# A second DMA queue for the stores and twiddle loads of one stage

## The chip, the cores and the metric

The kernel runs on one core of a Trainium2 chip: TensorE (PE in the profile) multiplies matrices, VectorE (DVE), ScalarE (ACT) and GpSimd (POOL) work on elements, and SyncE (SP) issues DMA transfers. ScalarE can issue them too, in the order of its own instructions. The transfers of every issuer run on the same 16 DMA engines of the core. The metric is the time of one execution on the device in microseconds.

## The reference, cut to what matters

```python
def attn(x, v, pos_emb, w1, w2):          # x, v: (2, 12480, 128); pos_emb: (12480, 64)
    h = (maximum(pos_emb @ w1, 0) @ w2) * exp(-0.01 * pos)[:, None]
    u = x * v
    U, H = rfft(u, n=2 * S, axis=1), rfft(h, n=2 * S, axis=0)
    y = irfft(U * H[None], n=2 * S, axis=1)[:, :S]
    return x * y
def moe(z, w_in, w_out):                  # z: (24960, 128); w_in: (128, 2048)
    g = z @ w_in
    return maximum(0.01 * g, g) @ w_out
out = moe(attn(...).reshape(24960, 128), moe_w_in, moe_w_out)
```

The long convolution is done by a Fourier transform of length 98 x 128, split into two short transforms with a multiplication by twiddles in the first; all of it in float32.

## The kernel before, in words

The work runs in this order: the first short transform of batch 0 and of the filter (0 to 176 us); the second transform of batch 0, the product with the filter, the way back and the preparation of the weights (176 to 357 us); then, for some 1440 us, the two matrix multiplications of the MLP over 64 tiles of tokens, with the convolution of batch 1 woven between them.

The change lies in the first part alone. It goes in 16 steps, c = 0 to 15, of four columns of the transform each (`MC = 4`). Step c does this:

- `load_a(c + 3)`: SyncE issues the load of the twiddles `ft` (L197), then x and v of batch 0 (`xt`, `vt`, through `load_tokens`, L67 and L69: one large transfer and two small ones for each). For every fourth step `load_pos` follows, with `pos` in the same way.
- The stores of step c - 1 (`store`, L287): two transfers of `o` to `scr1`, put off by one step in the list `late`, so that they stand behind the loads of step c + 3.
- `prep(c + 2)`: GpSimd multiplies x by v into `uh` (L212); VectorE and GpSimd turn `ft` by a fixed angle (L221, L235, L236) to make the second set of twiddles; TensorE transposes `pos` (L229), ScalarE copies it out (`pts`, L232), TensorE multiplies it by w1 (L240), VectorE puts the ReLU, times the window, into `uh` (L243).
- For each of the four columns: TensorE's products `a` (L314), ScalarE's copy of one half of it (`a1s`, L98), VectorE's sum and difference into `o` (L100, L102).

Buffers: `o` and `a1s` have two, `a`, `uh`, `xt` and `vt` three, `ft` five. Each engine runs its instructions in the written order, and an instruction that waits for a semaphore holds those behind it. Completions of DMA transfers are told by eight semaphores (DMAHW0 to DMAHW7) that are given out in turn over all issuers; a transfer whose semaphore is still held by an earlier one waits for that one's landing before it is issued.

At the end of the part, the last step's rows go to the tile `bin0` directly from `o` (L307), those of the other steps from `scr1` (L302), and the next part loads its tiles `bin` from `scr1` (L496), which needs every store to have landed.

The functions that the diff touches are these:

Of the kernel before, what the change touches and what calls it, by code (L numbers as in the profile page):

```python
# [20 lines left out]
MC = 4  # L21
# [6 lines left out]
def tile_conv_mlp(ctx, tc, x, v, pos_emb, w1, w2, w_in, w_out, cf, cr, cg, cb, ci, cw, out):  # L28
    nc = tc.nc
# [14 lines left out]
    scr1 = dram.tile([128, NA, 2 * C0], F32, name="scr1")  # L44
# [18 lines left out]
    def load_tokens(t, src, m0, n):  # L63

        full = src[: ROWS * NB, :].rearrange("(a p n) d -> a p n d", p=2, n=HB)
        for r in (slice(0, R0), slice(R0, ROWS)):
            nc.sync.dma_start(out=t[r], in_=full[r, :, m0:m0 + n, :])  # L67
        last = src[ROWS * NB + m0:ROWS * NB + m0 + n, :]
        nc.sync.dma_start(out=t[ROWS:], in_=last[None, None, :, :].to_broadcast([1, 2, n, last.shape[1]]))  # L69
# [24 lines left out]
    def add_sub(pool, a0, a1, dst0, dst1, view, bufs):  # L94

        a1s = pool.tile([128, 512], F32, tag="a1s", name="a1s", bufs=bufs)[:a1.shape[0]]
        n = a1.shape[1]
        nc.scalar.copy(a1s[:, :n], a1)  # L98
        yield
        nc.vector.tensor_tensor(out=dst0, in0=view(a0), in1=view(a1s[:, :n]), op=ALU.add)  # L100
        yield
        nc.vector.tensor_tensor(out=dst1, in0=view(a0), in1=view(a1s[:, :n]), op=ALU.subtract)  # L102

    def run(g):
        for _ in g:
            pass


    def chunk(c):
        k0 = c * KC  # L110
        return k0, min(KC, NA - k0)
# [46 lines left out]
    with tc.manual_schedule():  # L158
# [3 lines left out]
        def fetch_a(c):  # L162
            ft = s0.tile([128, MC1 * 4 * NA], F32, tag="s0", name="ft1", bufs=3)[:NA].rearrange(
                "a (m p e) -> a m p e", m=MC1, p=2)
            nc.sync.dma_start(out=ft, in_=cf[:, c * MC1:(c + 1) * MC1])
            xv = []
            for i, src in enumerate((x, v)):
                t = s0.tile([128, 1024], F32, tag=f"s{1 + i}", name="xv1", bufs=3 - i)[:NA, :2 * MC1 * D].rearrange(
                    "a (p m d) -> a p m d", p=2, d=D)
                load_tokens(t, src[1], c * MC1, MC1)  # L170
                xv.append(t)
            got[c] = ft, xv
# [3 lines left out]
        def mult_a(c):  # L176
            ft, (xt, vt) = got.pop(c)
            nc.gpsimd.tensor_tensor(out=xt, in0=xt, in1=vt, op=ALU.mult)
            u1[c] = ft, xt

        with ExitStack() as st:
# [9 lines left out]
            def load_pos(q):  # L191
                pos_t[q] = sba.tile([NA, 2, PQ, FO], F32, tag="pos", name="pos")
                load_tokens(pos_t[q], pos_emb, q * PQ, PQ)

            def load_a(c):
                ft = sba.tile([NA, MC, 2 * NA], F32, tag="ft", name="ft", bufs=5)
                nc.sync.dma_start(out=ft, in_=cf[:, c * MC:(c + 1) * MC, 0])  # L197
                xt = sba.tile([NA, 2, MC, D], F32, tag="xt", name="xt", bufs=3)
                vt = sba.tile([NA, 2, MC, D], F32, tag="vt", name="vt", bufs=3)
                load_tokens(xt, x[0], c * MC, MC)  # L200
                load_tokens(vt, v[0], c * MC, MC)
                f_t[c], xv_t[c] = ft, (xt, vt)
                if c < 2:
                    f1_t[c] = sba.tile([NA, MC, 2 * NA], F32, tag="f1", name="f1", bufs=3)
                    nc.sync.dma_start(out=f1_t[c], in_=cf[:, c * MC:(c + 1) * MC, 1])
# [45 lines left out]
            for i in range(2):  # L251
                nc.sync.dma_start(out=w1bd[64 * i:64 * i + 64, 64 * i:64 * i + 64], in_=w1)
            make_identity(nc, ident)
            load_a(0)
            nc.sync.dma_start(out=win, in_=cw)
            nc.sync.dma_start(out=rot, in_=cr)
            load_a(1)
            run(prep(0))
            load_a(2)
            run(prep(1))  # L260
            late = []
            for c in range(NC0):
                if c + 3 < NC0:
                    load_a(c + 3)
                    if (c + 3) * MC % PQ == 0:
                        load_pos((c + 3) * MC // PQ)
                if c == 2:
                    nc.sync.dma_start(out=mb, in_=cb)
                    nc.sync.dma_start(out=mi, in_=ci)
                    for s in range(2):  # L270
                        for ri in range(2):
                            nc.sync.dma_start(out=mi2[HB * s:HB * s + HB, ri], in_=ci[HB * ri:HB * ri + HB, s])
                if c == 6:
                    for m, mh, ml in ((mb.rearrange("p s r q -> p s (r q)"), mb_h, mb_l), (mi, mi_h, mi_l)):
                        nc.scalar.copy(mh, m)
                        nc.vector.tensor_tensor(out=ml, in0=m, in1=mh, op=ALU.subtract)
                for f in late:
                    f()
                late = []
                uh, ft, f1 = uh_t.pop(c), f_t.pop(c), f1_t.pop(c)  # L280
                nxt = prep(c + 2) if c + 2 < NC0 else iter(())
                o = sba.tile([NA, 2, MC, 2, C0], F32, tag="o", name="o")

                def store(m0, n, o, c=c):
                    for ri in range(2):
                        r0 = HB * ri + c * MC + m0
                        nc.sync.dma_start(out=scr1[r0:r0 + n].rearrange("m k e -> k m e"),  # L287
                                          in_=o[:, ri, m0:m0 + n].rearrange("a m s d -> a m (s d)"))
                if c == 7:
                    w22 = s0.tile([128, D], F32, tag="mi", name="w22", bufs=1)  # L290
                    for i in range(2):
                        nc.sync.dma_start(out=w22[64 * i:64 * i + 64, :], in_=w2)
                if c == NC0 - 3:
                    fetch_a(0)

                    bin0 = s0.tile([128, MC1 * 4 * NA], F32, tag="s0", name="bin0", bufs=3)[
                        :, :KC * 2 * C0].rearrange("p (k s e) -> p k s e", k=KC, s=2)

                def early():
                    for ri in range(2):  # L300
                        rows = slice(HB * ri, HB * ri + HB - DIR * MC)
                        nc.sync.dma_start(out=bin0[rows], in_=scr1[rows, :KC, :].rearrange("p k (s e) -> p k s e", s=2))  # L302

                def direct(m, o, c=c):
                    for ri in range(2):
                        r0 = HB * ri + c * MC + m
                        nc.sync.dma_start(out=bin0[r0:r0 + 1], in_=o[:KC, ri, m])  # L307
                if c == NC0 - 1:
                    mult_a(0)
                for mm in range(MC):  # L310
                    a = psa.tile([NA, 2, 512], F32, tag="a", name="a", bufs=3)
                    for p, f, n in ((0, ft, NA), (1, f1, ROWS)):
                        for ri in range(2):
                            nc.tensor.matmul(a[:, p, C0 * ri:C0 * ri + C0], f[:n, mm, NA * ri:NA * ri + NA],  # L314
                                             uh[:n, p, mm], start=True, stop=True)
                    run(add_sub(sba, a[:, 0, :2 * C0], a[:, 1, :2 * C0], o[:, :, mm, 0, :], o[:, :, mm, 1, :],
                                lambda t: t.rearrange("a (r e) -> a r e", r=2), 2))
                    next(nxt, None)
                    if c >= NC0 - DIR:
                        direct(mm, o)  # L320
                    if c == NC0 - 1 and mm == EARLY:
                        early()
                    if c == NC0 - 1 and mm == MC - 1:
                        store(0, MC, o)
                if c < NC0 - 1:
                    late.append(lambda store=store, o=o: store(0, MC, o))
# [161 lines left out]
        with ExitStack() as st:  # L488
# [111 lines left out]
            for c in range(NCH):  # L600
# [11 lines left out]
                n = chunk(c)[1]  # L612
# [234 lines left out]
```

## Time and profile before

| | |
|---|---|
| median of 3 runs | 1797.21 us (1795.04 to 1797.37) |
| the profiled execution | 1797.53 us, span 1795.5 us |
| PE, DVE, ACT, POOL busy | 95%, 54%, 50%, 33% of the span |
| first part, 0 to 176 us | PE 135.73, DVE 96.96, ACT 42.03, POOL 75.26 us busy; DMA share 0.90, 249 GB/s |

The whole-span shares are those of the long MLP part. The first part must be read alone, since other things limit it there. The DMA share is the mean busy share of the 16 DMA engines. In the rows `SPq` and `ACTq` are DMA-issuing and waiting instructions of SyncE and ScalarE, q1 is the DMA queue that SyncE issues into, q10 that of ScalarE. The tile `scr` stands for `scr1` here, and `o`, `xt` and so on leave out buffer numbers.

### The profile page before, as it was taken

The page shows a single profiled execution, that of the slowest core. Times are in us where ns is not written, and L with a number is a line of the kernel's source. Part 1 is how long each engine was busy: PE and PEld are TensorE (multiplying, and loading weights), DVE is VectorE, ACT ScalarE, POOL GpSimd, SP SyncE. Part 2 cuts the span into 40 slices and gives each one's busy share as a digit, 9 for nine tenths or more (in the row PEclk, how much of TensorE's full clock was granted, in tenths as well). Part 3 has the DMA queues.
Part 4 walks back from the last instruction along what each step waited for, and adds up shares of the span by engine and source line. Part 5 has one row for each costly group of instructions (what it writes and reads, how often), then busy time and mean ns, then how long its engine had stood idle before and what let it go on. Part 6 is the DMA issues. An engine that isn't in the chain of part 4 may idle for free.

```text
span 1795.5 us, 29288 instructions
## 1 busy us (share of the span) xinstructions
PE 1714.1 (95%) x10620; PEld 1607.7 (90%) x10620; DVE 966.5 (54%) x1688; ACT 892.5 (50%) x1803; POOL 587.2 (33%) x450
## 2 busy tenths in 40 slices
PE   6787989879999999999999999999999999999998
PEld 6677545479999999999999999999999999999998
DVE  3566788845455555555555544444444444444444
ACT  1222444324445666666666666444444444444444
POOL 3453334213323555555544444211121111211120
PEclk8789999989999999999999999999999999999999
DMA  9898999786756465555555541212211122112210
GB/s 224 244 274 259 310 301 321 235 248 192 216 159 180 121 179 142 140 144 144 144 144 144 141 129 54 77 50 65 60 50 50 54 64 57 51 50 60 65 51 14
DMA packets 147707, 251.77 MB, mean 140 GB/s; under 512 B 10842, under 2 KB 96742, under 8 KB 144492
## 3 DMA queue, kind: packets, MB, share of 16 engines
q1 hardware_dynamic: 127420, 224.21, 44.8%
q10 hardware_dynamic: 20144, 25.69, 4.3%
q8 instruction: 84, 1.38, 0.3%
q14 instruction: 59, 0.48, 0.1%
HBM read 166.37 MB, written 83.43 MB: 139 GB/s over the span
## 4 chain that ended last, share of the span: by engine, by line
PE 84%; DMA 9%; DVE 3%; SPq 2%; issue 1%; ACT 1%; POOL 0%; ACTq 0%; POOLq 0%; DVEq 0%
PE mh L693 10%; PE mh L695 10%; PE mh L694 10%; PE acc L713 10%; PE acc L712 10%; PE acc L714 10%; PE yp L679 6%; PE cv L132 4%; PE cv L350 2%; DMA scr<-o 2%; PE up L117 2%; PE dp L139 2%; DMA xt<-in_x_dram 2%; PE op L723 2%; DMA ft<-in_cf_dram 1%; PE xp L671 1%
## 5 line engine op out<-in xcount | busy, mean ns | idle before, releaser
L699 DVE SCALAR_TENSOR_TENSOR rl<-mh,rh 128x390 fp32r<-128x390 f32 x1024 | 574.9, 564 | 616.6 <-ACT rh L698 614.9
L698 ACT ACTIVATE rh<-mh 128x390 fp32r<-128x390 f32 x1024 | 508.1, 498 | 387.3 <-PE mh L695 369.9
L693 PE MATMUL mh<-zh,w_in_h 128*128 128x390 f32 x1024 | 366.0, 357 | 0.0
L695 PE MATMUL mh<-zh,w_in_l 128*128 128x390 f32 x1024 | 350.2, 342 | 0.0
L694 PE MATMUL mh<-zl,w_in_h 128*128 128x390 f32 x1024 | 349.4, 341 | 0.0
L713 PE MATMUL acc<-rl,w_out_h 128*128 128x390 f32 x1024 | 348.8, 341 | 0.0
L712 PE MATMUL acc<-rh,w_out_h 128*128 128x390 f32 x1024 | 348.3, 340 | 0.0
L714 PE MATMUL acc<-rh,w_out_l 128*128 128x390 f32 x1024 | 348.2, 340 | 0.0
L686 POOL TENSOR_TENSOR zl<-zf,zh 128x390 fp32r<-128x390 f32 x63 | 64.9, 1030 | 706.1 <-ACT zh L685 706.1
L693 PEld LDWEIGHTS mh<-zh,w_in_h 128*128 128x128 f32 x1024 | 194.0, 189 | 2.2 <-DVE rl L699 0.2
L694 PEld LDWEIGHTS mh<-zl,w_in_h 128*128 128x128 f32 x1024 | 193.9, 189 | 2.2 <-DVE zl L686 0.2
L695 PEld LDWEIGHTS mh<-zh,w_in_l 128*128 128x128 f32 x1024 | 194.0, 189 | 0.0
L713 PEld LDWEIGHTS acc<-rl,w_out_h 128*128 128x128 f32 x1024 | 193.9, 189 | 0.0
L714 PEld LDWEIGHTS acc<-rh,w_out_l 128*128 128x128 f32 x1024 | 193.1, 189 | 0.0
L712 PEld LDWEIGHTS acc<-rh,w_out_h 128*128 128x128 f32 x1024 | 193.0, 188 | 0.0
L679 PEld LDWEIGHTS yp<-g,cp 98*128 98x128 f32 x1024 | 123.5, 192 | 0.0
L679 PE MATMUL yp<-g,cp 98*128 98x97 f32 (+1 forms) x1024 | 123.1, 274 | 0.0
L431 POOL TENSOR_TENSOR us<-us,hd 128x512 f32<-128x512 f32 (+1 forms) x50 | 63.6, 1272 | 146.2 <-ACT us L429 146.2
L685 ACT CAST zh<-zf 128x390 fp32r<-128x390 f32 x64 | 33.2, 519 | 148.8 <-DVE zf L684 148.8
L485 POOL TENSOR_TENSOR cp<-cin 98x512 f32<-98x512 f32 x63 | 88.4, 1402 | 0.0
L484 POOL TENSOR_TENSOR cp<-cin 98x512 f32<-98x512 f32 x63 | 81.5, 1293 | 17.5 <-DMA cin<-scr 9.4
L98 ACT COPY a1s<-a 98x384 f32<-98x384 f32 x64 | 30.6, 479 | 110.3 <-PE a L314 67.2
(129 smaller groups left out, 2149.9 us busy)
## 6 DMA issues: line engine op xcount, KB each, us to landing
cin<-scr SPq DMA_DIRECT2D x63, 392.0 KB
hd<-hspec SPq DMA_DIRECT2D x48, 512.0 KB
g<-in_cg_dram SPq DMA_DIRECT2D x64, 300.1 KB
scr<-o SPq DMA_DIRECT2D x32, 588.0 KB
bin<-scr SPq DMA_DIRECT2D x23, 768.0 KB
scr1b<-o SPq DMA_DIRECT2D x32, 392.0 KB
hspec<-hs ACTq DMA_DIRECT2D x48, 256.0 KB
scr<-ct ACTq DMA_DIRECT2D x24, 512.0 KB
```

The source lines that it names most:

```text
L132: nc.tensor.matmul(dst, u, w, start=(i == 0), stop=(i == 2))
L484: eng.tensor_tensor(out=o1, in0=c0, in1=c1, op=ALU.subtract)
L485: eng.tensor_tensor(out=o0, in0=c0, in1=c1, op=ALU.add)
L679: nc.tensor.matmul(yp[:, at:at + n], ci_t[:, r, m, p, :], g[:, r, p, m, :n], start=(r == 0), stop=(r == 1))
L693: nc.tensor.matmul(hp, w_in_h[:, fs], zh, start=True, stop=False)
L694: nc.tensor.matmul(hp, w_in_h[:, fs], zl, start=False, stop=False)
L695: nc.tensor.matmul(hp, w_in_l[:, fs], zh, start=False, stop=True)
L698: nc.scalar.activation(out=rh, in_=hp, func=AF.Relu)
L699: nc.vector.scalar_tensor_tensor(out=rl, in0=hp, scalar=0.0, in1=rh, op0=ALU.max, op1=ALU.subtract)
L712: nc.tensor.matmul(ap, w_out_h[:, f, :], rh, start=False, stop=False)
L713: nc.tensor.matmul(ap, w_out_h[:, f, :], rl, start=False, stop=False)
L714: nc.tensor.matmul(ap, w_out_l[:, f, :], rh, start=False, stop=(f == NF - 1))
```

## The change

```diff
@@ load_a(c)
                 ft = sba.tile([NA, MC, 2 * NA], F32, tag="ft", name="ft", bufs=5)
-                nc.sync.dma_start(out=ft, in_=cf[:, c * MC:(c + 1) * MC, 0])
+                nc.scalar.dma_start(out=ft, in_=cf[:, c * MC:(c + 1) * MC, 0])
@@ store(m0, n, o, c=c)
                         r0 = HB * ri + c * MC + m0
-                        nc.sync.dma_start(out=scr1[r0:r0 + n].rearrange("m k e -> k m e"),
+                        nc.scalar.dma_start(out=scr1[r0:r0 + n].rearrange("m k e -> k m e"),
                                           in_=o[:, ri, m0:m0 + n].rearrange("a m s d -> a m (s d)"))
```

ScalarE issues 48 transfers that SyncE issued: 16 loads of `ft` and 32 stores. Everything else of the part stays with SyncE: x, v, pos, the second twiddles of steps 0 and 1 (`f`, L205), and constants. The instructions of TensorE, VectorE and GpSimd keep their order; the numbers of the semaphores they wait for change.

SyncE's order before, from the load of `ft` for step 8 to the stores of step 4:

```order
L197 DMA ft<-in_cf_dram 98x4x196 [waits DMAHW2_49,PE_49]
L67 DMA xt<-in_x_dram 96x2x512 [waits DMAHW3_49,Pool_49]
L67 DMA xt<-in_x_dram 1x2x512 [waits DMAHW4_49]
L69 DMA xt<-in_x_dram 1x2x512 [waits DMAHW5_49]
L67 DMA vt<-in_v_dram 96x2x512 [waits DMAHW6_49]
L67 DMA vt<-in_v_dram 1x2x512 [waits DMAHW7_49]
L69 DMA vt<-in_v_dram 1x2x512 [waits DMAHW0_49]
L67 DMA pos<-in_pos_emb_dram 96x2x1024 [waits DMAHW1_49]
L67 DMA pos<-in_pos_emb_dram 1x2x1024 [waits DMAHW2_49]
L69 DMA pos<-in_pos_emb_dram 1x2x1024 [waits DMAHW3_49]
L287 DMA scr_60<-o 98x4x384 [waits DMAHW4_49,DVE_49]
L287 DMA scr_60<-o 98x4x384 [waits DMAHW5_49]
```

SyncE's order now, from the load of x for step 8 to that for step 9:

```order
L67 DMA xt<-in_x_dram 96x2x512 [waits DMAHW2_49,Pool_49]
L67 DMA xt<-in_x_dram 1x2x512 [waits DMAHW3_49]
L69 DMA xt<-in_x_dram 1x2x512 [waits DMAHW4_49]
L67 DMA vt<-in_v_dram 96x2x512 [waits DMAHW6_49]
L67 DMA vt<-in_v_dram 1x2x512 [waits DMAHW0_49]
L69 DMA vt<-in_v_dram 1x2x512 [waits DMAHW2_49]
L67 DMA pos<-in_pos_emb_dram 96x2x1024 [waits DMAHW3_49,PE_49]
L67 DMA pos<-in_pos_emb_dram 1x2x1024 [waits DMAHW4_49]
L69 DMA pos<-in_pos_emb_dram 1x2x1024 [waits DMAHW5_49]
L67 DMA xt<-in_x_dram 96x2x512 [waits DMAHW0_49,Pool_49]
```

Of the twelve issues of such a step the load of `ft` and the two stores are gone; none of SyncE's waits in the step is for VectorE any more.

ScalarE's order in a later step without pos, as a piece of the difference (`pts` is the copy of the transposed pos, `a1s` that of a product):

```order
-L98 COPY a1s<-a 98x384 [waits DVE_49,PE_49,Activation_49] x4
+L98 COPY a1s<-a 98x384 [waits PE_49,Activation_49]
+L98 COPY a1s<-a 98x384 [waits DVE_49,PE_49,Activation_49] x2
+L197 DMA ft<-in_cf_dram 98x4x196 [waits DMAHW4_49,Pool_49]
+L287 DMA scr_60<-o 98x4x384 [waits DMAHW6_49,DVE_49]
+L287 DMA scr_60<-o 98x4x384 [waits DMAHW0_49]
+L98 COPY a1s<-a 98x384 [waits PE_49,Activation_49]
 L232 COPY pts<-pt 128x392 [waits PE_49]
```

Three issues now stand between the copy of a step's fourth product and that of the next step's first; the first store waits for VectorE, and each waits for an earlier transfer.

## Rows read from the trace of the kernel before

**Rows 1.** Timeline, VectorE: start us, us, engine, line, operation, out<-in, [idle before <-releaser].
```profile
43.00 0.56 DVE L100 TENSOR_TENSOR o<-a,a1s 98x384 f32<-98x384 f32 x1 [2.01 <-DMA scr<-o]
...
65.29 0.56 DVE L100 TENSOR_TENSOR o<-a,a1s 98x384 f32<-98x384 f32 x1 [2.57 <-DMA scr<-o]
...
70.56 0.54 DVE L102 TENSOR_TENSOR o<-a,a1s 98x384 f32<-98x384 f32 x1
...
86.60 0.56 DVE L100 TENSOR_TENSOR o<-a,a1s 98x384 f32<-98x384 f32 x1 [6.46 <-DMA scr<-o]
...
147.79 0.56 DVE L100 TENSOR_TENSOR o<-a,a1s 98x384 f32<-98x384 f32 x1 [2.59 <-DMA scr<-o]
```

**Rows 2.** Chain of waits from 43 to 147.8 us: shares by engine and line.
```profile
by line: DMA scr<-o 25.9%; DMA ft<-in_cf_dram 23.7%; PE a L314 14.4%; DMA xt<-in_x_dram 9.4%; DMA pos<-in_pos_emb_dram 7.7%; DMA vt<-in_v_dram 6.9%; SPq L67 4.6%; issue 3.0%; DVE o L102 3.0%; SPq L272 2.2%; PE hp L240 2.2%; DVE q L221 1.7%;
```

**Rows 3.** Busy time by stretch, as the first row names the columns.
```profile
core 0: us, PE busy (x) PEld busy (x) DVE busy (x) ACT busy (x) POOL busy (x), PEclk, DMA share, GB/s
...
43.00:147.80 104.80, 84.80 (x492) 77.67 (x490) 64.73 (x124) 26.12 (x57) 54.52 (x34) 0.85 0.93 262
```

**Rows 4.** Waits from 43 to 147.8 us: us in total, times, longest us.
```profile
DVE o L100 <- DMA scr<-o: 40.3, 11, 8.1
```

**Rows 5.** Timeline, SyncE's DMA issues around step 4's store.
```profile
68.67 0.33 SPq L197 DMA_DIRECT2D ft<-in_cf_dram  x1
...
74.03 2.48 SPq L67 DMA_DIRECT2D pos<-in_pos_emb_dram  x2
...
78.09 0.92 SPq L287 DMA_DIRECT2D scr<-o  x2
```

**Rows 6.** Timeline, VectorE and SyncE, the first and last of twelve stores.
```profile
40.45 0.55 DVE L102 TENSOR_TENSOR o<-a,a1s 98x384 f32<-98x384 f32 x1
...
49.63 1.01 SPq L287 DMA_DIRECT2D scr<-o  x2
...
140.00 6.04 SPq L287 DMA_DIRECT2D scr<-o  x4
...
144.66 0.54 DVE L102 TENSOR_TENSOR o<-a,a1s 98x384 f32<-98x384 f32 x1
```

**Rows 7.** Instructions by line: ns minimum/median/maximum, then first and last start.
```profile
L287 SPq DMA_DIRECT2D scr<-o x32: 308/358/1010, 34.9 to 169.3; - x32
...
L148 ACTq DMA_DIRECT2D scr<-ct x25: 364/366/398, 191.1 to 359.8; - x25
...
L98 ACT COPY a1s<-a x64: 478/478/482, 17.8 to 165.7; 98x384 f32<-98x384 f32 x64
```

**Rows 8.** DMA of five stretches: 43:147.8, 120:140, 156:161.5, 176:310, 228:240 us, in this order.
```profile
DMA packets 19123, 27.50 MB, mean 262 GB/s; under 512 B 1055, under 2 KB 14530, under 8 KB 19114
...
DMA packets 4407, 6.06 MB, mean 303 GB/s; under 512 B 206, under 2 KB 3496, under 8 KB 4405
...
DMA packets 1170, 1.76 MB, mean 320 GB/s; under 512 B 46, under 2 KB 1100, under 8 KB 1170
...
DMA packets 21475, 42.02 MB, mean 314 GB/s; under 512 B 1546, under 2 KB 12042, under 8 KB 21463
...
DMA packets 1846, 4.12 MB, mean 343 GB/s; under 512 B 150, under 2 KB 662, under 8 KB 1844
...
q1 hardware_dynamic: 740, 2.52, 65.6%
q10 hardware_dynamic: 1104, 1.57, 36.5%
```

**Rows 9.** Timeline, end of the stage: VectorE's last subtraction, SyncE's last issues.
```profile
166.67 0.55 DVE L102 TENSOR_TENSOR o<-a,a1s 98x384 f32<-98x384 f32 x1
...
168.75 0.98 SPq L287 DMA_DIRECT2D scr<-o  x2
...
175.04 0.82 SPq L496 DMA_DIRECT2D bin<-scr  x2
```

**Rows 10.** DMA issues of the whole execution: count, size of one.
```profile
scr<-o SPq DMA_DIRECT2D x32, 588.0 KB
```

## The prediction

> **What bounds the kernel now.** The change touches only batch 0's first stage, which takes the first 176 us of a span of 1795.5 us. So I read that stage alone. Its middle is the stretch from 43.00 to 147.79 us: VectorE starts its first add into `o` of step 2 and of step 13 there [rows 1], eleven steps of 9.53 us.
>
> First the chain of waits over this stretch [rows 2]. The reader is to see that five DMA entries stand for 25.9 + 23.7 + 9.4 + 7.7 + 6.9 = 73.6% of it, and TensorE's matmuls for 14.4%. Then the stretch by engine [rows 3]: the DMA engines are busy for 0.93 of it at 262 GB/s, VectorE for 64.7 of 104.8 us, ScalarE for only 26.1. By this alone the stage would be bound by DMA throughput, and a second queue would have nothing to win but 7%.
>
> The waits say more [rows 4]: VectorE loses 40.3 us, eleven times, to the landing of `scr<-o`. The tile `o` has two buffers, so step c may not write `o` before the stores of step c-2 have landed. Follow one case. VectorE ends step 4 at 70.56 + 0.54 = 71.10 us and is not let into step 6 before 86.60 [rows 1]. The stores of step 4 were ready to go at 71.10, but SyncE issued them at 78.09: it had ft at 68.67, x, v and then pos at 74.03 in front of them, each with its own wait for a completion semaphore [rows 5]. So 7.0 of these 15.5 us are queueing in SyncE's order, and 8.5 are the transfer itself. I did this for the stores of steps 1 to 12. The first of them is ready at 41.00 and issued at 49.63, 8.6 us late; the last is ready at 145.20 and is the second half of the four issues that begin at 140.00, 0.0 late [rows 6]. The twelve delays add up to 60.6 us, 5.05 each. From issue to landing a pair takes 7.8 us on the mean of eleven (the case above 8.5). VectorE's own part of a step is 71.10 - 65.29 = 5.8 us [rows 1]. Two steps are then 5.8 + 5.05 + 7.8 = 18.6 us, 9.3 for one, close to the measured 9.53. This loop, not the throughput, sets the pace, and the first of its terms that can go is the 5.05.
>
> **The change, part by part.**
>
> *The stores leave SyncE.* ScalarE issues them right behind its last copy of a step and waits there for VectorE's last subtraction. The 5.05 us of queueing go; what is left is a semaphore and the issue. With 0.5 us for that and 7.8 for the landing the loop is (5.8 + 0.5 + 7.8) / 2 = 7.05 us a step. It is then late no longer, and three others come up.
>
> *VectorE and ScalarE.* Three issues a step now stand in ScalarE's order. A store's issue takes 0.36 us on SyncE, and one of similar shape 0.37 us on ScalarE [rows 7]; 48 of them are some 18 us, beside ScalarE's idle 75% [rows 3], so the work itself is hidden. The order is not: the first copy of the next step stands behind the stores, and they stand behind VectorE's last subtraction. VectorE is idle for two issues and one copy, 2 x 0.37 + 0.48 [rows 7], with some 0.2 for semaphores 1.4 us. Its chain is 5.8 + 1.4 = 7.2 us a step. TensorE runs on meanwhile, since `a` has three buffers of the four products of a step.
>
> *DMA throughput.* The stretch moves 27.50 MB [rows 8]. What the engines can do with this mix in two queues no row of this stage shows, so I bound it. From below: the best 20 us of this stage in one queue, 303 GB/s, 90.8 us for the stretch. From above: 12 us of the next stage in which SyncE's queue loads ft, x, v and bin while ScalarE's queue stores, 343 GB/s, 80.2 us; there the shares of the two queues add to 65.6 + 36.5 = 102%, so they overlap a little. Stores alone come to 320 GB/s. I take 314, the mean of 134 us of two queues, since it is the longest stretch of that kind [rows 8]: 27.50 MB / 314 = 87.6 us, 8.0 a step. That is above 7.05 and 7.2, so throughput is late next. Saved: 104.8 - 87.6 = 17.2 us.
>
> *The ft loads leave SyncE.* They are three issues ahead of their use and have five buffers; nothing waits for the time of their issue. In the first 43 us both queues load at once; I count nothing for it, with 2 us either way, since pos and the first ft now share the engines.
>
> *New waits.* Both queues share eight completion semaphores, so a transfer's issue still waits for one issued about eight earlier, and on ScalarE copies are queued behind that wait. Counted in the built program, 8 of ScalarE's 48 issues wait for a store of the step before (or two before). A pair lands in 7.8 us and a step is 8.0, so such a wait is nearly over when it is reached: I take 0.4 us each, 3 us, with 0 and 8 as ends (8: one us each).
>
> *The end of the stage.* The last stores are issued at 168.75, 1.5 us after VectorE is done at 167.22, behind the direct copies of bin; the load of bin at 175.04 waits for them [rows 9]. That wait is the end of the chain into the next stage, so 1.5 us go. Behind 176 us nothing of the change is left, and the rest shifts as a whole.
>
> Sum: -17.2 + 3 - 1.5 = -15.7 us. The profiled execution took 1797.5 us (2 beyond its span), 0.3 above the median of 1797.2; 1797.2 - 15.7 = 1781.5 us. The ends: with 303 GB/s, 8 us of waits and 2 lost at the start, -14.0 + 8 + 2 - 1.5 = -5.5; with 343, no waits and 2 won, -24.6 - 2 - 1.5 = -28.1. So 1769 to 1792 for this case.
>
> **Rivals.**
>
> *A: the DMA engines are full already.* For: the share of 0.93 [rows 3]. Against: the same mix ran at 303 GB/s for 20 us, and the idle 7% are not all. If the packets take as long as now and only the gaps close, to a share of 0.97, the rate is 262 x 0.97 / 0.93 = 273 GB/s, 100.7 us: saved 4.1, less 3 for waits, plus 1.5: -2.6, 1794.6 us. The Trainium skill (DMA: Bandwidth & Descriptors, Issuing engines are not separate DMA queues) says this: queues of several engines run on the same 16 DMA engines, and a second issuer saves only the sequencer's time at issue. The trace agrees on the sharing (102% for both queues together). But the 5.05 us of [rows 5, 6] are just time at the issuer, which the rule leaves to be saved.
>
> *B: the stores land later and hold ScalarE.* Now a pair goes through at the full rate of its queue; beside SyncE's loads it may get half. A pair is 2 x 588 KB = 1.204 MB [rows 10]; at half of 303 GB/s that takes 7.9 us. The last pair, alone, took 175.04 - 168.75 = 6.3 us [rows 9], of which 1.204 MB at 320 GB/s are 3.8, so some 2.5 are fixed. Together 10.4 us. The wait of a store for the store of the step before then makes a step at least 10.4 + 0.4 = 10.8 us long: 11 x 10.8 = 118.8, 14 us more than now, 12.5 more with the end of the stage: 1809.7 us. It decides from the point where a pair needs more than about 9.1 us from issue to landing. Against: loads that are finished early leave the engines to the stores, and bytes bound the stretch all the same. The Trainium skill (DMA: Bandwidth & Descriptors, Queues, rings and completion order) has each DMA engine take turns between the queues that have work, packet by packet, which is the half share. The trace agrees so far as both queues are served in the same 12 us, with 65.6% and 36.5% [rows 8]; no run here shows what a store loses by it.
>
> *C: the queues don't part.* SyncE's loads still wait, through the eight semaphores, for stores issued on ScalarE; if this holds them to the old order, the time stays at 1797. Against: the stores themselves no longer stand behind the loads.
>
> **How the numbers follow.** Forecast 0.62, A 0.16, B 0.17, C 0.05. A measurement of this kernel tells about 0.2%, 3.6 us, from no change. Of the forecast's range all is faster; A at -2.6 is mostly within, a third of it beyond; C is within. So faster 0.62 + 0.05 = 0.67, same 0.11 + 0.05 = 0.16, slower 0.17. The range: the forecast's own, 1769 to 1792, holds some 0.55; it is drawn to 1768 below and to 1804 above, which takes in A, C and the half of B in which fewer steps are held.
>
> **What would show it.** Right: SyncE's queue (q1) and a second (q10) side by side before 150 us at over 300 GB/s together; the stores' issues within 1 us of VectorE's last subtraction; VectorE's waits for `scr<-o` down from 40 to under 15 us; steps of about 8.0 us; the load of bin that ends the stage near 160 us instead of 175; all behind it moved as a whole. Step by step wrong: if the rate stays near 273 GB/s it is A. If ScalarE's queue shows waits of several us for DMA ahead of L287 or L197, VectorE waits for `a1s`, and a pair lands in 9 us or more, it is B. If the stage is shorter but the total is not, the next stage, which is near its own DMA limit, took it back; I give that no chance of its own, as its work and transfers are the same.

## The result: slower, 1814.0 us against 1797.3

The changed kernel takes 1813.98 us (median of four runs, 1809.87 to 1818.48), the kernel before 1797.29 on the same chip: a ratio of 1.0097, 95% interval 1.0079 to 1.0114, some 17 us. The profiled execution has a span of 1816.6 us, 21.1 more than before.

Where the time went is read from the same stretch as before, from VectorE's first add of step 2 to that of step 13. First VectorE's timeline (columns as in [rows 1]):

```profile
45.27 0.56 DVE L100 TENSOR_TENSOR o<-a,a1s 98x384 f32<-98x384 f32 x1 [1.46 <-ACT a1s L98]
...
163.38 0.56 DVE L100 TENSOR_TENSOR o<-a,a1s 98x384 f32<-98x384 f32 x1 [1.71 <-ACT a1s L98]
```

The eleven steps take 118.1 us, 10.74 each, where they took 104.8 and 9.53 [rows 1]; the forecast had 8.0. So 13.3 us are lost here and 2.3 ahead of it. Busy time in that stretch (columns of [rows 3]):

```profile
45.27:163.38 118.11, 91.28 (x496) 84.75 (x496) 72.94 (x124) 25.75 (x59) 57.94 (x35) 0.84 0.84 251
```

The DMA engines fell from a share of 0.93 to 0.84 and from 262 to 251 GB/s. Two queues leave them idler, not fuller. Over the busy share that is 251 / 0.84 = 299 GB/s, against 262 / 0.93 = 282: the packets go no slower. The DMA view of the stretch shows that the queues did part (answers to [rows 8]):

```profile
DMA packets 19828, 29.69 MB, mean 251 GB/s; under 512 B 1128, under 2 KB 14446, under 8 KB 19819
...
q10 hardware_dynamic: 13126, 16.53, 46.0%
q1 hardware_dynamic: 6693, 13.05, 37.4%
```

The waits of the stretch, engine by engine (columns of [rows 4]), say who stands still:

```profile
SPq L67 <- DMA scr<-o: 13.6, 6, 3.7
...
SPq L67 <- DMA ft<-in_cf_dram: 4.5, 2, 4.2
SPq L69 <- DMA scr<-o: 4.3, 3, 2.9
...
ACT a1s L98 <- DMA ft<-in_cf_dram: 16.4, 4, 5.1
ACT a1s L98 <- DMA scr<-o: 12.5, 4, 5.0
...
DVE o L100 <- ACT a1s L98: 40.7, 21, 6.3
...
PE hp L240 <- ACT pts L232: 17.4, 8, 3.6
PE pt L229 <- DMA pos<-in_pos_emb_dram: 10.9, 3, 7.1
...
POOL uh L212 <- DMA vt<-in_v_dram: 14.4, 3, 6.4
POOL uh L212 <- DMA xt<-in_x_dram: 13.6, 3, 6.6
```

VectorE's 40.3 us of waiting for `scr<-o` [rows 4] are gone; 40.7 us for ScalarE's copy `a1s` stand in their place. ScalarE waits at its issues for transfers to land, 16.4 + 12.5 = 28.9 us in these two rows. And SyncE, in front of loads of x, v and pos (L67, L69), waits for `scr` and ft, which ScalarE issues. GpSimd then waits for v and x, TensorE for pos. The chain of waits from 62 to 100 us shows one place where SyncE stands for ScalarE (start us, us, what):

```profile
71.24 9.45 DMA scr<-o
...
80.71 0.61 SPq L67
...
83.24 10.05 DMA pos<-in_pos_emb_dram
...
93.34 0.56 PE pt L229 x4
```

A store that ScalarE issued at 71.24 lands at 80.69. Until then SyncE, idle from 76.95 on, may not issue its load of v (80.71), since that load takes the store's semaphore; pos stands behind it, is issued at 83.24 and lands when TensorE begins to transpose it. A second place, in the timeline of all engines (answers to [rows 5, 6]), shows ScalarE held:

```profile
136.75 0.33 ACTq L197 DMA_DIRECT2D ft<-in_cf_dram  x1
...
137.85 0.55 DVE L102 TENSOR_TENSOR o<-a,a1s 98x384 f32<-98x384 f32 x1
...
141.27 0.82 ACTq L287 DMA_DIRECT2D scr<-o  x2
141.68 1.96 SPq L67 DMA_DIRECT2D vt<-in_v_dram  x2
142.19 0.48 ACT L98 COPY a1s<-a 98x384 f32<-98x384 f32 x1 [5.07 <-DMA ft<-in_cf_dram]
...
143.11 2.03 PE L240 MATMUL hp<-w1bd,pts 128*98 128x128 f32 x8 [3.61 <-ACT pts L232]
```

VectorE has finished the step at 138.40, but ScalarE issues the store at 141.27. It takes the semaphore of ScalarE's own second store of the step before, which was issued at 131.35 and landed at 141.19; the ft that the row of the next copy names is another semaphore in that copy's list and had not landed in full by then. So the split of ScalarE's waits between ft and `scr` is not to be relied on, their sum is. SyncE's load of v at 141.68 waits here for one of its own, the load of v issued at 131.39. The copy of the next step, the copy of the positions and TensorE's `hp` stand behind ScalarE's wait. The chain over the stretch (answer to [rows 2]) begins with `scr` still, and pos has come up to second place:

```profile
by line: DMA scr<-o 30.8%; DMA pos<-in_pos_emb_dram 14.5%; PE a L314 14.3%; PE hp L240 6.3%; DMA vt<-in_v_dram 4.5%; DMA xt<-in_x_dram 4.2%; issue 4.0%; SPq L67 3.5%; ACTq L287 3.4%; ACT a1s L98 2.6%; DMA ft<-in_cf_dram 2.6%; DVE o L102 2.6
```

The end of the stage (answers to [rows 9]) is the timeline of both queues:

```profile
180.74 1.06 ACTq L287 DMA_DIRECT2D scr<-o  x2
...
181.97 6.06 SPq L307 DMA_DIRECT2D bin<-o  x4
189.80 0.83 SPq L496 DMA_DIRECT2D bin<-scr  x2
```

The load of bin comes at 189.80 instead of 175.04, 14.8 us late: from step 13 to it passed 26.4 us, 0.8 less than before. But among the four direct copies there, L307, is one more wait. The instructions of that line, as in [rows 7]:

```profile
L307 SPq DMA_DIRECT2D bin<-o x8: 572/582/2331, 177.5 to 187.5; - x8
```

The last one goes 6.7 us after VectorE's end (it was 0.9): one of the copies takes 2.33 us to issue instead of 0.58, which no run explains, and the one ahead of the last, at 186.84, is held 1.9 us for the semaphore of a store that ScalarE issued at 180.74. So the next stage's first `ep` starts 18.6 us late (190.2 against 171.6), and the first product of the last stage (L679) 22.0 us late. Of the 21 us of the two profiled executions the 4 beyond the medians' 17 are within the spread of the runs.

### The profile page after: what moved, and what is told of

Its sections match the earlier page's. It is cut to its first block, busy times and chain, and to the rows that moved or that the text cites. A ratio compares the mean times of both kernels' runs of the same rounds, so it can differ in the third digit from the quotient of the medians.

```text
span 1816.6 us, 29292 instructions
## 1 busy us (share of the span) xinstructions
PE 1723.6 (95%) x10620; PEld 1617.6 (89%) x10620; DVE 977.5 (54%) x1688; ACT 892.2 (49%) x1803; POOL 591.0 (33%) x450
## 4 chain that ended last, share of the span: by engine, by line
PE 86%; DMA 7%; DVE 4%; issue 1%; ACT 1%; SPq 1%; ACTq 0%; POOL 0%; POOLq 0%
PE mh L693 10%; PE mh L695 10%; PE mh L694 10%; PE acc L713 10%; PE acc L712 10%; PE acc L714 10%; PE yp L679 6%; PE cv L132 4%; DMA scr<-o 3%; PE cv L350 3%; PE up L117 3%; PE dp L139 2%; PE op L723 2%; DMA pos<-in_pos_emb_dram 1%; PE xp L671 1%; PE a L314 1%
## 5 line engine op out<-in xcount | busy, mean ns | idle before, releaser
L679 PEld LDWEIGHTS yp<-g,cp 98*128 98x128 f32 x1024 | 125.1, 194 | 0.0
L679 PE MATMUL yp<-g,cp 98*128 98x97 f32 (+1 forms) x1024 | 124.7, 275 | 0.0
L98 ACT COPY a1s<-a 98x384 f32<-98x384 f32 x64 | 30.6, 482 | 121.2 <-PE a L314 64.1
L484 POOL TENSOR_TENSOR cp<-cin 98x512 f32<-98x512 f32 x63 | 81.5, 1294 | 17.4 <-DMA cin<-scr 17.4
```

The lines of the kernel that those rows point to most:

```text
L484: eng.tensor_tensor(out=o1, in0=c0, in1=c1, op=ALU.subtract)
L679: nc.tensor.matmul(yp[:, at:at + n], ci_t[:, r, m, p, :], g[:, r, p, m, :n], start=(r == 0), stop=(r == 1))
```

## Experiments

Each time is the median of four executions, for e10, e15 to e17 and e19 to e21 of ten; the ratio is that to the kernel before on the same chip, with its 95% interval. Four theories are named in the expectations: H1, ScalarE's copies stand behind the stores in its order; H2, a transfer lands later since two queues share the engines; H3, ScalarE is held by the waits of its ft issues; H4, formed after the first four kernels, is about SyncE: the eight completion semaphores go round over both queues, so a load on SyncE waits until a transfer has landed that ScalarE issued late. In the trace of the changed kernel 38 of SyncE's 140 issues up to the load of bin take a semaphore that a transfer of ScalarE used last.

**Each half of the change alone, and the order alone.**

```
e1: only the stores are nc.scalar.dma_start
e2: only ft is nc.scalar.dma_start
```

> ScalarE issues the 32 stores, SyncE the ft loads again. Theory H1 (order: what costs is that ScalarE's copies a1s and pts stand behind the stores' waits, so that TensorE starves): the stores still hold the copies, most of the loss stays: 1806 to 1814 us. Theory H2 (landing: two queues share the DMA engines, a pair of stores lands in some 10 us instead of 7.8 and the step can be no shorter): the second queue carries 1.2 of 1.5 MB a step, the same 1806 to 1814. A third, H3 (the waits of the ft issues for completion semaphores hold ScalarE): 1797 or less.

> ScalarE issues the 16 ft loads, SyncE the stores again. H1: no wait for VectorE stands on ScalarE any more, only the semaphore waits of ft: 1794 to 1800 us. H2: the stores are back in the queue of the loads and land in about 8 us: 1795 to 1799. H3 (ft's waits): most of the loss stays, 1806 to 1814.

e1: 1812.26 us, ratio 1.0091 [1.0076, 1.0106]. e2: 1825.29, 1.0169 [1.0152, 1.0187]. The stores alone cost what the whole change costs, as H1 and H2 had it, and ft alone costs more, which no theory had. Why the two together cost no more than the stores alone is not shown. SyncE's waits of e2 from 0 to 195 us:

```profile
SPq L67 <- DMA ft<-in_cf_dram: 36.9, 8, 7.5
SPq L287 <- DMA ft<-in_cf_dram: 7.7, 2, 5.9
```

No other engine has a wait for ft there, and ScalarE stands at its issues for one landing alone, 2.1 us for an x: H3 falls. It is SyncE that stands still for ft, before its loads. That is H4. Transfers that land later (H2) do not explain it: by the updates of their semaphores the large loads of x take 7.1 us from issue to landing on the mean of steps 2 to 12 (8.0 before) and those of v 4.9 (6.3), a store 6.6 (6.0).

```
-                    load_a(c + 3)          (and pos)      # e3, all on SyncE
                 for f in late:             # stores of c-1
                     f()
+                    load_a(c + 3)
```

> The kernel before, all on SyncE, with the stores of step c-1 issued ahead of the loads for step c+3 instead of behind them. The loop theory of the prediction (the 5.05 us a store queues in SyncE's order set the pace): steps go from 9.5 to about 8.3 us, 1785 to 1790 us, VectorE's wait for scr<-o far below 40 us. If the DMA engines bound the stage instead: 1794 to 1799.

1817.56, 1.0125 [1.0105, 1.0144], in neither range. In this one-queue kernel the stores no longer queue behind loads, and the wait that the forecast was built on is gone: 3.6 us are left of it. Waits of e3, 0 to 195 us:

```profile
SPq L287 <- DVE o L102: 29.5, 12, 6.3
...
POOL uh L212 <- DMA vt<-in_v_dram: 73.2, 10, 19.0
...
DVE o L100 <- DMA scr<-o: 3.6, 3, 2.6
```

But SyncE now waits for VectorE with the loads behind it, v comes late, and 22 us are lost. So this order takes away the 5.05 us of queueing [rows 5, 6] and wins nothing: what holds SyncE ahead of its loads costs more here than the queueing did.

**ScalarE's order.**

```
e4 (after): the stores of c-1 go behind column 1 of step c
e5 (after): the copy pts of step c+2 goes ahead of the stores of c-1
```

> The changed kernel, but ScalarE issues the stores of step c-1 behind the second column of step c, so that two a1s copies and the pts copy stand ahead of them. H1: TensorE no longer waits for pts behind a store: 1785 to 1798 us. H2: a pair still lands in 10 us, is issued 3 us later, and VectorE waits for it again: (5.8 + 3 + 10) / 2 = 9.4 to 10 us a step, 1798 to 1812.

> The changed kernel with the copy of the transposed positions (pts of step c+2) ahead of the stores of step c-1 in ScalarE's order. H1: TensorE's wait for that copy (24 us in all) goes, and with it half the loss: 1800 to 1808 us. H4: SyncE and ScalarE still wait for the same landings: 1810 to 1816.

e4: 1819.28, 1.0128 [1.0110, 1.0147], in neither range. ScalarE's wait for landings of stores falls from 27.7 to 11.2 us (0 to 195 us), and it is slower: SyncE waits longer instead for what ScalarE issues later (62.5 us for ft and `scr` against 44.8). e5: 1811.08, 1.0084 [1.0063, 1.0105], 3 us below the change, which the two intervals do not tell apart. TensorE's waits in e5, 20 to 190 us:

```profile
PE pt L229 <- DMA pos<-in_pos_emb_dram: 24.0, 3, 8.7
...
PE hp L240 <- ACT pts L232: 1.8, 1, 1.8
```

Its wait for the copy is gone and one for pos, a load of SyncE, is there instead. So little is won by ScalarE's order alone.

```
+                    def wait_dve(o=o):                    # e17, before
+                        tw = sba.tile([NA, 1], F32, tag="tw", name="tw", bufs=2)
+                        nc.scalar.copy(tw, o[:, 1, MC - 1, 1, :1])
+                    late.append(wait_dve)
                     late.append(lambda store=store, o=o: store(0, MC, o))
```

> The kernel before, all transfers on SyncE, plus a copy of one column by ScalarE (98 x 1, from the last result of VectorE in step c-1) at the very place where the changed kernel's stores stand in ScalarE's order: three copies of a, this, the fourth copy of a, the copy of the positions. It takes nothing away; ScalarE's output of that copy is read by nobody. H1 (the copies that follow wait behind VectorE's end): 1805 to 1815 us, as with the stores there. H4 (semaphores of transfers): 1793 to 1799, as before, since no transfer moves.

1795.20, 0.9995 [0.9985, 1.0005]. In ScalarE's waits the copy does what the stores' wait for VectorE does (0 to 195 us), and it costs nothing:

```profile
ACT tw L328 <- DVE o L102: 33.4, 15, 8.1
```

H1 in its plain form falls, with the loads issued as early as before.

**Semaphores of their own.** The eight semaphores go round over SyncE's and ScalarE's transfers, not over all issuers as was said ahead: in the trace of e10 the transfers of GpSimd complete on eight others.

```
e10 (before): ft is nc.gpsimd.dma_start
e11 (before): the stores are nc.gpsimd.dma_start
```

> The kernel before with the twiddles' loads issued by GpSimd, whose transfers complete on semaphores of their own; x, v, pos_emb and the stores on SyncE. H4: with the shared semaphores out of it, a second queue costs little: at most 1803 us, against 1825 with the same loads on ScalarE. H2 (two queues): 1820 to 1830, as on ScalarE. H3 (the issuing engine is held by its waits): GpSimd has the differences of the positions to compute, so a delay of its own could show as VectorE waiting for GpSimd; 1797 to 1815.

> The kernel before with the stores of batch 0's first stage issued by GpSimd, on semaphores of their own. H4 and H1 alike: neither SyncE's loads nor ScalarE's copies wait for a store, 1780 to 1800 us, against 1812 with the stores on ScalarE. H2: 1808 or more. What speaks against a gain: GpSimd's differences for the step after next stand behind the store's wait for VectorE.

e10: 1793.19, 0.9980 [0.9967, 0.9993]. The same loads in a second queue cost 30 us on ScalarE and nothing on GpSimd: H2 falls for ft. Besides the semaphores the queue is of another kind there (q0 software_dynamic on the page, q10 hardware_dynamic for ScalarE), and GpSimd's own order stands ahead of the issue; the waits of SyncE are what points at the semaphores. SyncE's waits for ft from 0 to 195 us are down to this row:

```profile
SPq L287 <- DMA ft<-in_cf_dram: 0.6, 1, 0.6
```

e11: 1808.66, 1.0090 [1.0060, 1.0119]; I had expected 1780 to 1800. It doesn't test the semaphores, for GpSimd became late itself (waits from 20 to 175 us, then VectorE's `q` from 20 to 160 us, in e11 and in the kernel before):

```profile
DVE f L236 <- POOL q L221: 25.0, 7, 6.3
...
POOL scr L287 <- DVE o L102: 42.2, 16, 3.2
```

```profile
L221 DVE TENSOR_TENSOR q<-ft,rot 98x784 f32<-98x784 f32 x14 | 34.4, 2458 | 2.9 <-DMA ft<-in_cf_dram 2.9
L221 DVE TENSOR_TENSOR q<-ft,rot 98x784 f32<-98x784 f32 x14 | 14.9, 1067 | 3.7 <-DMA ft<-in_cf_dram 3.7
```

GpSimd stands 42.2 us at the stores, the factors `f` come late, and VectorE's product `q` takes 2458 ns on the mean, 1067 before (why is told at the end).

**Fewer transfers on the eight.** First the short loads of x and v are merged, 7 transfers a step instead of 9:

```
+    def load_two(t, src, m0, n):            # in place of load_tokens for x and v
+        full = src.rearrange("b s d -> (b s) d")[: NA * NB, :].rearrange("(a p n) d -> a p n d", p=2, n=HB)
+        for r in (slice(0, R0), slice(R0, NA)):
+            nc.sync.dma_start(out=t[r], in_=full[r, :, m0:m0 + n, :])
e6: in the changed kernel; e7: in the kernel before; e18: e7 with ft on ScalarE
```

> The control: the kernel before with the same merged loads, everything on SyncE. All theories: about the same as before or a little faster, 1788 to 1797 us, by some 20 transfers of one row that are no longer issued. It counts as the base of the kernel above.

> The changed kernel with the two short loads of x and of v merged: a step of batch 0 issues 7 transfers (5 loads, 2 stores), where it had 9. H4 (the eight completion semaphores are handed out in order over both queues, so SyncE's load waits for a transfer that ScalarE has yet to issue): eight semaphores then reach past a whole step, SyncE is held less, and the distance to its control, the kernel before with the same merged loads, shrinks to under 9 us from 17; about 1798 to 1806 us. H1 (what costs is that ScalarE's copies stand behind the stores' waits in its own order): the distance stays 14 to 20 us; 1805 to 1814. H2 (a transfer lands later since two queues share the engines): the distance stays, since bytes and queues are the same.

> The twiddles' loads alone on ScalarE, with the short loads of x and v merged: 7 transfers a step, so that the one that waits for a twiddles' landing stands a step on. H4: the loss against the kernel before with the same merged loads (1788 us) shrinks from 30 us to under 20; at most 1808. Any other theory keeps it: 1814 to 1820.

e7: 1787.85 us, 0.9960 [0.9944, 0.9976]. e6: 1805.27, 1.0055 [1.0036, 1.0073], still 17.4 above its control e7. e18: 1816.40, 1.0119 [1.0099, 1.0139], 28.5 above. Both of H4's numbers missed. SyncE's waits of e18, 0 to 195 us, show why:

```profile
SPq L75 <- DMA ft<-in_cf_dram: 32.6, 6, 8.9
SPq L293 <- DMA ft<-in_cf_dram: 17.0, 4, 6.9
```

The merged loads took transfers off the eight but no waits off SyncE: the round of eight now ends on other instructions, and the stores (L293) wait for ft as well. Which issue meets a late landing seems to count for more than how many transfers a step has; that is argued from these rows.

Then ft is issued for a later step:

```
-                    load_a(c + 3): ft of c+3 ahead of x and v        # e2
+                late = []
+                if c + 4 < NC0:
+                    load_ft(c + 4)                                  # e12, on ScalarE as well
```

> The twiddles' loads alone on ScalarE (1825 us where they stand with step c's loads of x and v), but each is issued a step earlier in ScalarE's order, behind the stores of the step before; the order in which the semaphores go round is nearly the same. H4 (SyncE is held until a transfer has landed that ScalarE issues late): most of the loss goes, 1790 to 1803 us, and SyncE's waits for ft fall from 36 us to under 12. H1 and H3 (ScalarE is held by the issue's own waits): 1818 or more, since the issue now stands ahead of four more columns' copies. H2 (two queues): 1820 to 1830.

1823.74, 1.0158 [1.0134, 1.0182]: as e2, and far from H4's 1790 to 1803. As built, ft stands where it stood in ScalarE's order, behind three copies of `a` in each step, so an earlier issue was not tested. But each ft is there a step ahead of its use now, and the loss stays: it is not ft that is late for its readers.

Then more of the loads go to GpSimd's semaphores, in pairs of which one has the stores or ft on ScalarE:

```
e15: e7 with ft and v as nc.gpsimd.dma_start; x, pos and stores on nc.sync
e16: e15 with the stores on nc.scalar         e19: e15 with ft on nc.scalar
e21: e15 with pos on nc.gpsimd                e20: e21 with the stores on nc.scalar
```

> The control of the kernel below: merged short loads of x and v, the twiddles and v issued by GpSimd on semaphores of their own, x, pos_emb and the stores by SyncE: 1780 to 1800 us by all theories (GpSimd issues three transfers of 0.75 us more a step).

> The same with the stores on ScalarE. SyncE and ScalarE now issue four or five transfers a step, so that one that is eight earlier is two steps old: no store waits for a store of the step before, and no load for a store that ScalarE has not long issued. H4 (waits for the transfer eight earlier, in both engines, are what the change costs): within 5 us of the control above, or faster. H1 (ScalarE's copies stand behind the stores' wait for VectorE): 10 to 20 us slower than the control. H2 (transfers of two queues land later): 10 to 20 us slower as well, with stores landing later than 9 us.

> The same with v on GpSimd, on semaphores of its own: 5 transfers a step are left on the eight. H4: within 7 us of the kernel that has the twiddles and v on GpSimd (1789), so at most 1796. Otherwise 1810 or more.

> Control of the kernel below: merged short loads, the twiddles, v and pos_emb on GpSimd with its own semaphores, x and the stores on SyncE. 1782 to 1795 us by all theories.

> The same with the stores on ScalarE. Four transfers a step are left on the eight semaphores, so a transfer waits for one two steps old, which has to have landed anyway before VectorE may write that buffer of o. H4 in its present form (what costs is SyncE and ScalarE waiting, at an issue, for a landing of the other queue or of the step before): within 4 us of the control, and ScalarE's wait for a store under 8 us, against 27 with pos_emb on SyncE. Otherwise (the 0.8 us of two issues a step and VectorE's end ahead of ScalarE's copies, or transfers of more queues landing later): 8 us or more above the control.

One thing more moved in e13, e15, e16 and e18 to e21: batch 1's loads of the same twiddles (`ft1`, L163 to L165), 17 issues of which the first falls into this stage. They are issued where ft is, on GpSimd, in e18 and e19 on ScalarE. The pairs e16/e15 and e20/e21 have them alike on both sides; e18 and e19 differ in them from their controls. So the table has, beside the loss by the medians, the loss up to the next stage's first `ep`, from one profiled execution of each.

e15: 1788.77, 0.9965 [0.9954, 0.9976]; e16: 1798.66, 1.0022 [1.0010, 1.0034]; e19: 1802.24, 1.0035 [1.0021, 1.0049]; e21: 1795.79, 1.0004 [0.9991, 1.0018], just outside its range; e20: 1800.77, 1.0029 [1.0013, 1.0045]. The three losses are between H4's numbers and the others' (e16's at the edge of the others') and smaller than with the same transfers on ScalarE and 9 on the eight. The last columns of the table are sums over the rows of the waits view, 0 to 195 us, for landings of ft and of `scr`: SyncE's, as kernel / control, and ScalarE's (no control has any).

| on ScalarE, transfers a step on the eight | control | loss, us | loss up to `ep`, us | SyncE's waits, us | ScalarE's waits, us |
|---|---|---|---|---|---|
| e2: ft, 9 | before | 30 | 28.6 | 52.8 / 22.4 | 0 |
| e12: ft, 9 | before | 29 | 28.4 | 52.5 / 22.4 | 2.8 |
| e18: ft, 7 | e7 | 28.5 | 23.3 | 61.3 / 27.4 | 3.6 |
| e19: ft, 5 | e15 | 13.5 | 8.2 | 45.7 / 7.8 | 0 |
| e1: stores, 9 | before | 17 | 16.5 | 51.6 / 22.4 | 30.6 |
| e6: ft and stores, 7 | e7 | 17.4 | 21.5 | 52.6 / 27.4 | 34.7 |
| e16: stores, 4 to 5 | e15 | 9.9 | 10.0 | 24.7 / 7.8 | 27.0 |
| e20: stores, 4 | e21 | 5.0 | 5.0 | 17.9 / 9.7 | 26.9 |

For e20 I had expected under 8 us of ScalarE waiting for stores. Its row:

```profile
ACT a1s L104 <- DMA scr<-o: 26.9, 8, 8.9
```

That miss tells much. Against e1, ScalarE waits almost as long, and the loss fell from 17 to 5 us; with ft alone ScalarE hardly waits and 30 are lost. The traces of e20 and e21 say where the 5 us are: steps 2 to 13 take 98.4 and 98.8 us, so the loop loses nothing. The last direct copy (L313) goes 6.8 us after VectorE's end in e20 and 2.3 in e21 (two of the copies take 2.0 and 2.4 us to issue, 0.6 in e21; why is not shown), and `ep` follows 5.0 us later.

But e16 points to a cost of ScalarE's waits as well. Steps 2 to 13 take 102.6 us there and 96.3 in its control e15, 6.3 more, and no load of SyncE waits for a store in that stretch. It is ScalarE that stands at its issues, and VectorE behind it (44.9 to 147.5 us):

```profile
DVE o L106 <- ACT a1s L104: 22.6, 10, 5.3
...
PE hp L246 <- ACT pts L238: 15.8, 10, 4.6
ACT a1s L104 <- DMA scr<-o: 15.5, 5, 4.1
ACT a1s L104 <- DMA xt<-in_x_dram: 7.7, 2, 6.0
```

So SyncE's waits of the table don't set the loss either. In e6, e16 and e20 12 to 13 us of them stand ahead of a direct copy that could not go before VectorE was ready, and cost nothing; without them the stores' four rows have an excess over the control of 29 (e1), 12 (e6), 4 (e16) and -4 us (e20), and a loss of 16.5, 21.5, 10.0 and 5.0. e19 has 38 us of excess and lost 8.2 up to `ep`; there v does not stand behind SyncE.

```
e13: e7 with ft as nc.gpsimd.dma_start, all else on nc.sync
```

> Merged short loads, the twiddles on GpSimd, all else on SyncE: if what the two gave apart adds up (9 and 2 to 4 us), 1780 to 1787 us; if both shorten the same queue ahead of the stores, 1785 to 1790.

1787.55, 0.9947 [0.9932, 0.9963]. It and e7 beat both kernels and cannot be told apart (their intervals overlap): the merged loads make the gain, and the second queue for ft adds nothing that shows.

What is shown: both engines stand at their issues for earlier transfers to land. With ft alone it is SyncE, before its loads, at a cost of 30 us, and on GpSimd's queue the same loads cost none. What stays open: with the stores on ScalarE, in the changed kernel too, how much is SyncE's standing still and how much ScalarE's; and how much of e16's, e19's and e20's smaller loss is due to v and pos being off SyncE. In e21 SyncE already waits 70.6 us for VectorE ahead of the stores, so it has time to spare there. H4's number held for e5, e10 and e17 and missed for e6, e11, e12, e16, e18, e19 and e20. A kernel with semaphores set by hand was not tried.

## Why the prediction was wrong

The step that failed is *New waits*, 3 us in the sum. SyncE's waits for landings of ft and `scr` went from 22.4 to 44.8 us (0 to 195 us), ScalarE's from none to 44.1, and a step took 10.74 us instead of 8.0. The two queues share their semaphores, and both engines stand for them. ft alone shows SyncE's side of it at a cost of 30 us (e2); in e16, where no load of SyncE waits for a store, 6.3 us go with ScalarE's. How the 13.3 us of the changed kernel's stretch divide between them is open. Step by step:

*What bounds the kernel now.* The loop over `o`, two buffers and 9.3 us a step, fitted the 9.53 and was taken for the cause. e3 takes its queueing away in one queue and loses 22 us. The row [rows 4] was where the lateness of all engines came together, not what could be shortened. Right was that VectorE's wait for `scr<-o` goes, and that the stores are issued about 0.5 us behind VectorE's last subtraction: 0.5 on the mean of steps 1 to 12, 2.9 at most.

*The ft loads leave SyncE, cost nothing.* Those who use ft do not wait for it, though it is only one step ahead of VectorE's and GpSimd's product (L221) and three ahead of TensorE's use alone. But the issues of SyncE wait, through the semaphores, a term that was put at nothing. Alone the move costs 30 us (e2), with semaphores of their own 0 or less (e10).

*New waits.* I counted 8 issues of ScalarE that wait for a store of the step before and took 3 us. That was too few for ScalarE, which waited 44.1 us, and it looked at one direction. SyncE has 38 issues that take the semaphore of a transfer of ScalarE; the prediction named this in rival C and priced it at "the old order", 1797 us, with 0.05. C's mechanism is the one that ft alone bears out, with a wrong price: in the old order SyncE issued the transfer and the later load itself, one after the other; now the first stands behind ScalarE's copies and VectorE's last subtraction.

*DMA throughput, 314 GB/s.* It never became the limit: 251 GB/s were moved, at a share of 0.84. Rival A falls by the same row. The Trainium skill (DMA: Bandwidth & Descriptors, Issuing engines are not separate DMA queues) grants a second issuer only the sequencer's time at issue. With ft on GpSimd 0.2% was won (e10), which agrees; that the 5.05 us were such time to be saved, as the prediction had it, no run bore out.

*VectorE and ScalarE.* 1.4 us a step were allowed for the order, with "TensorE runs on meanwhile, since `a` has three buffers". VectorE waited 40.7 us for `a1s` in the eleven steps, 3.7 a step. TensorE did not run on: the copy `pts` for `hp` stands behind the stores too (17.4 us in the stretch). But e5 won 3 us at most by another order, and in e17 a wait at the same place cost nothing.

*Rival B* came nearest in time, 1809.7 us and 10.8 us a step against 10.74, and in the landing: stores took 7.3 to 9.8 us in the chain of the changed kernel, around the 9.1 from which it decides; on the mean of steps 2 to 12 a single store landed 7.1 us after its issue, 6.0 before. Its signs (VectorE waits for `a1s`, ScalarE for landings) are all in the profile. Its mechanism, ScalarE held by late stores, is at work too, as at 141.27, and in e16 6.3 us go with it. Yet ft alone loses more without it, and in e20's loop ScalarE stands 13.6 us for stores (45 to 143 us) and nothing is lost. B had no wait of SyncE, and no term for ft. So that its step came out at 10.8 is in part luck.

*The end of the stage*, -1.5 us: 0.8 were won up to the load of bin, and 3.8 lost at the direct copies on SyncE: one waits 1.9 us for a store's semaphore, another takes 1.8 us longer to issue.

## What to carry to other kernels

Here a second queue on ScalarE parted the issues but not the completion semaphores: where these go round over both queues, each queue can wait for landings of the other, and the queue that feeds the kernel can be held by the later issuer (e2), as can the compute engine that issues (e16). Before moving transfers to a compute engine, list for every issue of the queue that stays which transfer its semaphore waits for, and when that one will be issued after the move. A wait that everybody meets, like that for a buffer, need not be the one to shorten: a run that removes it in one queue is a cheap test.

## What the runs showed of the hardware

Merging two short loads of one row each into one, for x and for v, won 0.4% (e7), though it moves the same bytes: 32 issues of 0.57 us fewer on SyncE in the stage. How much of the gain is their time and how much the changed round of semaphores is not shown. And a GpSimd that works beside VectorE's products slowed them. From e11's timeline of both:

```profile
104.61 5.15 DVE L221 TENSOR_TENSOR q<-ft,rot 98x784 f32<-98x784 f32 x1
104.90 2.36 POOL L212 TENSOR_TENSOR uh<-xt,vt 98x1024 f32<-98x1024 f32 x1
107.23 1.70 POOL L221 TENSOR_TENSOR q<-ft,rot 98x784 f32<-98x784 f32 x1
...
114.53 0.96 DVE L221 TENSOR_TENSOR q<-ft,rot 98x784 f32<-98x784 f32 x1
```

The product takes 0.96 us alone and 5.15 beside two instructions of GpSimd, whose 2.36 + 1.70 us make up nearly all of the difference of 4.19. The two of GpSimd take no longer than in the kernel before (2.41 and 1.72 on the mean): VectorE waits, though its record starts 0.29 us ahead. The Trainium skill (SBUF — State Buffer, Who interferes with whom) says that a VectorE instruction with two inputs in SBUF contends with a GpSimd instruction that reads SBUF, since its second input comes through the read interface that the two share, and that this sharing is an exclusive lock. This trace agrees: VectorE gets nowhere while either of the two runs.
